# Five more score pairs on VectorE in the first five head groups of a fused attention and long-convolution kernel

## The chip, the cores and the metric

One core of one Trainium2 chip runs the whole program. The metric is the device time of one execution in microseconds; the profile gives the span of one execution of the same kernel, which is about 2 us shorter. Five engines work side by side, each on its own list of instructions that it takes strictly in order: TensorE (PE in the profile; its weight loads are PEld), ScalarE (ACT), VectorE (DVE), GpSimd (POOL) and SyncE (SP), which issues most DMA transfers. Engines wait for each other on semaphores. PSUM, where TensorE writes its results, has eight banks of 128x512 fp32.

## The reference, cut to what matters

Two branches over S = 2048 tokens with D = 640 channels are mixed by a gate. Branch B is attention with 32 query heads of 20 channels that share one key and one value head. Branch A is a short convolution of `A_k` (4 taps), a product with `A_v`, a long convolution along the 2048 tokens done as Fourier transforms, and a product with `A_q`.

```python
def _B_ref(x, wq, wk, wv, wo):
    q = (x @ wq).reshape(B, S, 32, 20)        # per head
    k, v = x @ wk, x @ wv                     # one head, shared
    p = softmax(q k^T * 20 ** -0.5)           # 32 x 2048 x 2048 scores
    return (p v).reshape(B, S, 640) @ wo

def _A_ref(q, k, v, shift_k, ssm_k, ssm_D):
    kv = short_conv4(k, shift_k) * v
    y = irfft(rfft(kv, 2S) * rfft(ssm_k, 2S))[:S] + kv * ssm_D
    return q * y

g = sigmoid((x * gate_w).sum(-1))
out = g * _A_ref(x, ...) + (1 - g) * _B_ref(x, ...)
```

The scores are 32 x 2048 x 2048 exponentials. The kernel cuts them into 2048 tiles of 128 keys x 512 queries for one head.

## The kernel before

**Groups and tiles.** A head group `G` (32 of them) is four heads for one block of 512 queries. It has 16 key blocks `j`, and each (G, j) has four tiles, one for each head `r`. A tile's scores come from one matmul with 20 (+1) channels of 32 rows, so up to four tiles with different `r` use different row strips of the array at once. ScalarE takes the exponential of three tiles (`ETA`, 128x1536) and of two tiles (`ETB`, 128x1024) by turns, out of PSUM banks 0-2 and 3-4. TensorE then multiplies the exponentials with the values (the PV matmuls, into bank 6).

**Pairs on VectorE.** In some (G, j), the list `DVE_J[G]` says which, two of the four tiles are not given to ScalarE. VectorE computes their exponentials with a polynomial on the bits of the number.

```python
SIDE = (7, 5)
DVE_J = [()] * 5 + [(3, 8, 13)] * 27
...
    def stream(self):
        tiles, self.on_dve, self.pv_order = [], {}, []
        order = (0, 1, 2, 3)
        for G in range(8 * NB):
            for j in range(NSC):
                mine = order
                if j in DVE_J[G]:
                    mine, rest = order[:2], order[2:]
                    self.on_dve[G, j] = tuple(sorted(rest))
                    order = rest + mine
                self.pv_order.append((G, j, mine))
                tiles += [(G, j, r) for r in mine]
        self.units, i = [], 0
        while i < len(tiles):
            n = 2 if len(self.units) % 2 else 3      # ETB, ETA by turns
            self.units.append(tiles[i:i + n])
            i += n
...
        def DEXP(G, j):                              # one pair on VectorE
            ...
            for h, r in enumerate(rs):
                gr = self.group("dqk", pr, banks=(5, 7))
                gr.rides = True                      # scores beside another score group
                self.mm(gr, ...score(e, bk, G, j, r)...)
                self.evac(gr, "dve", ...W <- bank * a + b...)      # L1120, 128x512, twice
            V(... X <- (w + DP) * w ...)                           # L1123, 128x1024
            V(... X <- (X + DQ) * w ...)                           # L1124, 128x1024
            V(... ETd (int16 bits) <- X * DA + W ...)              # L1126, 128x1024
...
            if j == 0:                               # in PV, after the first key block of G
                for jd in DVE_J[G]:
                    DEXP(G, jd)
                    a = PVmm(ra, jd, T["ETd"][:, 0:512], ...)
                    b = PVmm(rb, jd, T["ETd"][:, 512:1024], ...)   # both before PV of G's last j
```

`dW` has two buffers, `dX` and `ETd` have one.

**The order is made beforehand.** All operations are recorded in a graph with estimated costs. A list scheduler places them, engine by engine, when its own estimates say that the inputs, a PSUM bank and the gap until the next score group allow it; it fills gaps on TensorE with side work (projections, the short convolution, the Fourier transforms) or with dummy matmuls. What comes out is a fixed list for each engine. On the chip each engine follows its list, and waits where an estimate was too short.

```python
    def kshift(self):                                # the short convolution
        for b in range(NB):                          # 4 blocks of 512 tokens
            x = self.g.add("sp", ...e.dma_start_transpose(kTr block b, A_k block b)..., lat=1.6)  # L1293
            x.iss = 3.3
            self.dma(kv block b, A_v block b)
        ...
        for c in range(NDC):
            for q in range(NB):                      # 16 matmuls of 128x128x128 per (c, q), L1310
                ... matmul(bank, kTr[:, c, t0:t0 + 128], kdiag[:, c, j, :]) ... reads kTr blocks q and q - 1
                self.evac(gr, "dve", ...kv <- bank * kv...)
```

In the list before, the first matmul that needs the second block of `kTr` stands behind the scores of the 10th exponential; the first that needs the third block stands behind those of the 17th, and the first that needs the fourth block behind those of the 20th.

Of the kernel before, what the change touches and what calls it, by code (L numbers as in the profile page):

```python
# [541 lines left out]
UP = 256.0  # L542

SIDE = (7, 5)
DVE_J = [()] * 5 + [(3, 8, 13)] * 27
MAC_ALT = ()
SCALE = float(DH) ** -0.5

# [25 lines left out]
class Kernel:  # L574
# [451 lines left out]
    def stream(self):  # L1026
# [4 lines left out]
# [5 lines that stand above are left out]
# [11 lines left out]
    def attention(self):  # L1047
# [88 lines left out]
        def PV(G, j, rs, more=False):  # L1136
# [13 lines left out]
            if j == 0:  # L1150
                for jd in DVE_J[G]:
                    DEXP(G, jd)
# [418 lines left out]
```

## Time and profile before

| what | before |
|---|---|
| time, median of 3 | 893.52 us (893.17 to 894.32) |
| span of the profiled execution | 891.6 us |
| ScalarE busy | 868.3 us, 97% |
| TensorE busy | 855.1 us, 96% |
| VectorE busy | 658.2 us, 74% |
| GpSimd busy | 365.6 us, 41% |
| exponentials on ScalarE | 378 `ETA` and 377 `ETB`; the last `ETA` holds one tile |
| pairs on VectorE | 81 |
| dummy matmuls on TensorE (L1511) | 916, 75.8 us |

The page gives for each engine the time in which it had an instruction under way. For ScalarE the recorded start of an exponential can lie before the end of the one ahead of it, so that durations overlap (378 times a mean of 1570 ns and 377 times 1151 ns are more than the span); what one costs is the distance between ends. TensorE's share contains the dummy matmuls and matmuls that run at once in different strips.

### The profile page before, as it was taken

To read this page: it belongs to the slowest core of one execution; us is meant where nothing else is said; L and a number is where in the kernel's file an instruction comes from. 1 tells how busy PE (TensorE), PEld (TensorE's weight loads), DVE (VectorE), ACT (ScalarE), POOL (GpSimd) and SP (SyncE) were. 2 spreads that over 40 slices of the span, in tenths; PEclk is the share of its full clock that TensorE was granted. 3 is DMA by queue.
4 is the path that set the end of the run, shared out by engine and by line. 5 is a ranking of instruction groups with operands and counts; after the bars stand their busy time and mean duration, and the time that the engine had idled before them with its cause. 6 is when DMAs were issued, how large, how long until landed. Compare 5 with 4: busy or idle time off the path is not lost.

```text
span 891.6 us, 17952 instructions
## 1 busy us (share of the span) xinstructions
PE 855.1 (96%) x7801; PEld 348.9 (39%) x7825; DVE 658.2 (74%) x867; ACT 868.3 (97%) x779; POOL 365.6 (41%) x311
## 2 busy tenths in 40 slices
PE   7899999999999999999999999999999999999997
PEld 3334434433433344433333334443444443343233
DVE  6457653298778788877879877768887678878674
ACT  5899999999999999999999999999999999999995
POOL 2950057860333377244427324268512677300000
PEclk9999999999999999999999999999999999999999
DMA  7930200010000011000001010000000000300211
GB/s 158 210 128 11 67 20 15 19 31 19 21 13 20 12 28 31 20 20 14 18 10 42 20 48 23 19 9 19 19 20 19 14 14 2 101 22 29 65 43 53
DMA packets 58371, 32.62 MB, mean 37 GB/s; under 512 B 41139, under 2 KB 54324, under 8 KB 58292
## 3 DMA queue, kind: packets, MB, share of 16 engines
q1 hardware_dynamic: 56026, 30.89, 12.5%
q8 instruction: 61, 1.00, 0.5%
q10 hardware_dynamic: 2266, 0.59, 0.3%
q14 instruction: 18, 0.15, 0.1%
HBM read 17.85 MB, written 6.02 MB: 27 GB/s over the span
## 4 chain that ended last, share of the span: by engine, by line
ACT 79%; PE 17%; DMA 2%; SPq 1%; DVE 1%; issue 0%; DVEq 0%
ACT ETA L1091 47%; ACT ETB L1091 32%; PE ps L1368 5%; PE ps L1059 5%; PE ps L1131 3%; PE ps L1310 1%; PE ps L982 1%; DMA kTr<-in_A_k_dram 1%; DMA xT<-in_A_q_dram 1%; SPq L755 1%; PE ps L1434 0%; SPq L1293 0%; PE ps L1511 0%; PE ps L1249 0%; DVE ETd L1126 0%
## 5 line engine op out<-in xcount | busy, mean ns | idle before, releaser
L1091 ACT ACTIVATE ETA<-ps 128x1536 bf16<-128x1536 f32 x378 | 593.4, 1570 | 3.9 <-PE ps L1059 3.4
L1091 ACT ACTIVATE ETB<-ps 128x1024 bf16<-128x1024 f32 x377 | 433.9, 1151 | 0.1
L1401 POOL TENSOR_TENSOR Pp<-X,K 128x512 f32<-128x512 bf16 x120 | 180.2, 1528 | 373.7 <-DVE K L1389 373.6
L1059 PE MATMUL ps<-qT,kT 32*128 32x512 bf16 x2048 | 300.2, 385 | 20.4 <-ACT ETA L1091 13.1
L1059 PEld LDWEIGHTS ps<-qT,kT 32*128 32x128 bf16 x2048 | 73.8, 91 | 255.4 <-ACT ETB L1091 121.7
L1131 PE MATMUL ps<-ETA,vaug 128*32 128x512 bf16 x1132 | 152.7, 385 | 0.0
L1120 DVE TENSOR_SCALAR dW<-ps 128x512 f32<-128x512 f32 x162 | 111.3, 687 | 50.7 <-PE ps L1059 49.4
L1131 PE MATMUL ps<-ETB,vaug 128*32 128x512 bf16 x754 | 148.5, 385 | 0.1
L1126 DVE SCALAR_TENSOR_TENSOR ETd<-dX,dW 128x1024 int16<-128x1024 f32 x81 | 110.6, 1366 | 25.3 <-PE ps L1131 25.0
L1123 DVE SCALAR_TENSOR_TENSOR dX<-dW 128x1024 f32<-128x1024 uint16 x81 | 111.7, 1380 | 0.9
L1124 DVE SCALAR_TENSOR_TENSOR dX<-dX,dW 128x1024 f32<-128x1024 f32 x81 | 108.7, 1341 | 0.5
L1401 POOL TENSOR_TENSOR AB<-Pp 128x256 bf16<-128x256 f32 x80 | 82.1, 1026 | 6.0
L1434 PE MATMUL ps<-AB,Tcos 128*128 128x256 bf16 x320 | 77.3, 275 | 0.0
L1511 PE MATMUL ps<-Tcos,zeros 128*32 128x512 bf16 x916 | 75.8, 385 | 0.3
L1434 PE MATMUL ps<-AB,Tsin 128*128 128x256 bf16 x280 | 68.6, 274 | 0.0
L1401 POOL TENSOR_TENSOR Pp<-Pp 128x512 f32<-128x512 f32 x40 | 61.0, 1524 | 3.1
L1368 PE MATMUL ps<-ssm_kT,Tcos 128*128 128x256 bf16 x320 | 55.3, 276 | 0.0
L1368 PE MATMUL ps<-kv,Tcos 128*128 128x256 bf16 x320 | 50.2, 275 | 0.1
L1368 PE MATMUL ps<-ssm_kT,Tsin 128*128 128x256 bf16 x320 | 49.1, 274 | 0.0
L1368 PE MATMUL ps<-kv,Tsin 128*128 128x256 bf16 x320 | 48.4, 274 | 0.0
L1131 PEld LDWEIGHTS ps<-ETA,vaug 128*32 128x32 bf16 x1132 | 29.3, 94 | 34.9 <-issue 34.0
L982 PE MATMUL ps<-xT,wq_pad 128*128 128x512 bf16 x137 | 38.9, 382 | 2.5 <-issue 1.3
(137 smaller groups left out, 746.8 us busy)
## 6 DMA issues: line engine op xcount, KB each, us to landing
rbc<-scr_d SPq DMA_DIRECT2D x31, 256.0 KB
scr_o<-oTn SPq DMA_DIRECT2D x24, 128.0 KB, 1.7
xn<-in_A_q_dram SPq DMA_DIRECT2D x4, 640.0 KB
kv<-in_A_v_dram SPq DMA_DIRECT2D x4, 640.0 KB, 4.8
out_dram<-outsb SPq DMA_DIRECT2D x14, 160.0 KB, 1.8
oTp<-scr_o SPq DMA_DIRECT2D x12, 160.0 KB, 2.8
wog<-in_B_wo_dram SPq DMA_DIRECT2D x4, 200.0 KB
wo<-in_B_wo_dram SPq DMA_DIRECT2D x4, 200.0 KB
```

The costliest lines, as they stand in the source:

```text
L982: o = self.mm(gr, lambda e, bk, gi=gi, dc=dc: e.matmul(self.bank(bk), T["wq_pad"][:, dc, 128 * gi:128 * gi + 128], T["xT"][:, dc, 512 * I: ...
L1059: return e.matmul(self.bank(bk), T["kT4"][32 * r:32 * r + 32, 128 * j:128 * j + 128], T[f"qT{G // 8 % 2}"][32 * r:32 * r + 32, G % 8, :], ...
L1091: op("act", lambda e: e.activation(et(n)[:, 0:w], self.ps[:, lo:lo + w], ACT.Exp, scale=SCALE), [("ps", base[n % 2] + k) for k in range(le ...
L1120: self.evac(gr, "dve", lambda e, bk, h=h: e.tensor_scalar(W[:, 512 * h:512 * h + 512], self.bank(bk), SCALE * LOG2E * 128.0, 128.0 * (127 ...
L1123: V(lambda e: e.scalar_tensor_tensor(X[:, :], w, DP, w, ALU.add, ALU.mult), [kW], ["dX"], c_ps(1024), **k)
L1124: V(lambda e: e.scalar_tensor_tensor(X[:, :], X[:, :], DQ, w, ALU.add, ALU.mult), [kW], ["dX"], c_ps(1024), **k)
L1126: V(lambda e: e.scalar_tensor_tensor(T["ETd"][:, :].bitcast(dt.int16), X[:, :], DA, W[:, :], ALU.mult, ALU.add), [kW, "dX"], ["ETd"], c_ps ...
L1131: return op("pe", lambda e: e.matmul(self.bank(6)[32 * r:32 * r + 32, :], T[va][:, j, :], src, start=(j == 0), stop=(j == NSC - 1), tile_p ...
L1368: self.mm(gr, lambda e, bk, lhs=lhs, rhs=rhs, comp=comp, n=n: e.matmul(self.bank(bk, 256, 256 * comp), lhs, rhs, start=(n == 0), stop=(n = ...
L1401: f = lambda e: e.tensor_tensor(out, a, b, alu)
L1434: self.mm(gr, lambda e, bk, lhs=lhs, fc=fc, comp=comp, h=h: e.matmul(self.bank(bk, 256, 256 * h), lhs, AB[:, fc, :, comp, :], start=(fc == ...
L1511: sch.filler = [[lambda e, r=r, st=st: e.matmul(self.bank(6)[32 * r:32 * r + 32, :], self.T["zeros"][:, 0:32], self.T["Tcos"][:, 0, 0:512] ...
```

## The change

Each of the first five head groups, which had no pair on VectorE, gets one, at key block 6. The aim is to take ten of the 2048 tiles off ScalarE. Everything else in the source stays as it is; the scheduler then makes new lists for all engines.

```diff
--- before.py
+++ after.py
@@ -542,7 +542,7 @@
 UP = 256.0
 
 SIDE = (7, 5)
-DVE_J = [()] * 5 + [(3, 8, 13)] * 27
+DVE_J = [(6,)] * 5 + [(3, 8, 13)] * 27
 MAC_ALT = ()
 SCALE = float(DH) ** -0.5
 
```

The new lists hold 375 full `ETA`, one `ETA` of one tile and 375 `ETB` on ScalarE, five times five more instructions of a pair on VectorE, and the same 2048 score matmuls on TensorE. In the new TensorE list the first matmul that needs the second block of `kTr` stands behind the scores of the 12th exponential, the first that needs the third block behind those of the 16th, and the first that needs the fourth block behind those of the 20th. SyncE's list is the same up to and with the three `xn` loads behind the `kTr` transposes. The last 66 rows of the TensorE list (the last score groups and the output projection) are the same, instruction by instruction.

## Prediction, made before the run

> **What bounds the kernel now.** I read the busy shares first, then the chain that ended last, then the chain in order of time, the list of ScalarE's instructions, and at last the stages.
>
> ```profile
> PE 855.1 (96%) x7801; PEld 348.9 (39%) x7825; DVE 658.2 (74%) x867; ACT 868.3 (97%) x779; POOL 365.6 (41%) x311
> ...
> ACT 79%; PE 17%; DMA 2%; SPq 1%; DVE 1%; issue 0%; DVEq 0%
> ACT ETA L1091 47%; ACT ETB L1091 32%; PE ps L1368 5%; PE ps L1059 5%; PE ps L1131 3%; PE ps L1310 1%; PE ps L982 1%; DMA kTr<-in_A_k_dram 1%; DMA xT<-in_A_q_dram 1%; SPq L755 1%; PE ps L1434 0%; SPq L1293 0%; PE ps L1511 0%; PE ps L1249 0%; DVE ETd L1126 0%
> ```
>
> Two engines look full, but 75.8 us of TensorE are dummies, and the chain is ScalarE's exponentials for 79% of the span. From the chain in order of time, near the end:
>
> ```profile
> 845.41 1.34 ACT ETA L1091
> 846.75 0.92 ACT ETB L1091
> 847.67 1.34 ACT ETA L1091
> ```
>
> This is the pitch with nothing in the way: 1.34 us for three tiles, 0.92 for two, 2.26 for five. The 1570 and 1151 ns in the page's groups are recorded durations that overlap, so I don't use them. 377 x 2.26 = 852.0, plus the one-tile `ETA` (0.50 in the chain) is 852.5. The first exponential starts at 23.98, the chain puts the end of the last at 882.1: 858.1 us. So about 5.6 us are lost between exponentials. I followed the ends (start plus duration) of all 755 in the list of ScalarE's instructions against that pitch. The places:
>
> ```profile
> 32.94 1.53 ACT L1091 ACTIVATE ETA<-ps 128x1536 bf16<-128x1536 f32 x1
> 34.27 1.12 ACT L1091 ACTIVATE ETB<-ps 128x1024 bf16<-128x1024 f32 x1
> 37.71 1.45 ACT L1091 ACTIVATE ETA<-ps 128x1536 bf16<-128x1536 f32 x1 [2.32 <-PE ps L1059]
> 39.23 1.02 ACT L1091 ACTIVATE ETB<-ps 128x1024 bf16<-128x1024 f32 x1
> 40.56 1.45 ACT L1091 ACTIVATE ETA<-ps 128x1536 bf16<-128x1536 f32 x1 [0.31 <-PE ps L1059]
> ```
>
> Between 35 and 47 us some 3.1 us are lost (2.4 in the first gap, then 0.17, 0.42 and 0.12); between 100 and 180 about 1.3 in pieces of 0.1 to 0.2; between 460 and 740 about 0.9. A duration of 1.45 for an `ETA` is one whose scores had only just come; 1.72, seen near 80 us, is one whose scores lay ready. What made the first gap, from TensorE's instructions in order of time and from the chain:
>
> ```profile
> 35.72 1.35 PE L1310 MATMUL ps<-kdiag,kTr 128*128 128x128 bf16 x11 [1.75 <-DMA kTr<-in_A_k_dram]
> 37.00 0.61 PE L1059 MATMUL ps<-qT,kT 32*128 32x512 bf16 x3
> ```
>
> ```profile
> 27.70 7.96 DMA kTr<-in_A_k_dram
> ```
>
> TensorE, in order, came to a short-convolution matmul whose block of `kTr` had not landed; the scores of the 11th exponential stood behind it. By stage (columns: length, then busy time of PE, PEld, DVE, ACT, POOL, granted clock, DMA):
>
> ```profile
> 35.50:39.00 3.50, 3.29 (x25) 2.18 (x25) 1.07 (x2) 1.29 (x1) 3.50 (x7) 0.51 1.24 257
> ...
> 80.00:170.00 90.00, 89.23 (x816) 41.01 (x814) 43.08 (x83) 89.86 (x81) 41.03 (x39) 1.00 0.11 27
> ```
>
> After the wait TensorE ran at half clock. From 80 to 170 us ScalarE is busy throughout and TensorE has under 1 us free in 90, while VectorE is at 48%. That is the stage that gets the new pairs, and the chain of waits does run over TensorE in it; still ScalarE loses little there.
>
> [...] L1123, L1124 and L1126 have medians of 1219 to 1224 ns. [...] the same three run up to 2174 to 2176 ns, with means of 1341 to 1380. [...]
>
> **The change, part by part.**
>
> *ScalarE.* Ten tiles go: 2048 - 2 x 81 = 1886 tiles become 1876. In fives that is 377 rounds and one tile before, 375 rounds and one tile after. Two rounds less: 2 x 2.26 = 4.5 us. The rest of one tile is the same, so the end of the kernel keeps its shape. The whole of it lies on the path.
>
> *VectorE.* Five pairs more, each two evictions (L1120, 687 ns mean) and three passes at 1.22 to 1.37 us: 5.0 to 5.5 us, 25 to 27 in all, over the first 150 us or so. VectorE's work there was about half of the time (48% from 80 to 170, 78% in the busiest 20 us), so it rises to some 70%, under the 79% that it has from 190 to 880, where three pairs in a group cost ScalarE almost nothing. I count 0.
>
> *TensorE.* The same score and PV matmuls. A pair's scores ride beside another score group; its two PV matmuls (385 ns each, side by side) make a batch of their own, and I count 0.3 us for it with the break in the batches, 1.5 for five; four score groups less give about 4 x 0.3 = 1.2 back. Net near 0. But the stage from 80 to 170 is dense, so the side work is pressed into slightly less ScalarE time: I put down 0.3 us of new small losses.
>
> *The order.* The lists are made anew, and this is worth as much as the sum above is uncertain. `kTr` lands by SyncE's list, unchanged that far. Block two was issued at 27.70 and landed at 35.67, 7.96 later. Blocks three and four were issued at 32.76 and 38.19; with the same 7.96 they land at about 40.7 and 46.2 (an estimate: before, TensorE first needed them at 45.04 and 48.30, without a wait). In the new list:
> - Block two is needed behind the scores of the 12th exponential instead of the 10th, one round later: about 36 instead of 33.96. It has then landed. The gap of 2.3 us goes.
> - Block three is needed behind the 16th. Without the gap those scores are issued when the 14th exponential ends, at 23.98 + 7 x 2.24 = 39.7, so TensorE arrives at about 40.3 and waits 0.4, which the buffered scores hide.
> - Block four is needed behind the 20th: 23.98 + 9 x 2.24 = 44.1, so TensorE arrives at about 44.5 and waits about 1.7. Nine matmuls (0.6) and the scores (0.35) follow, so the 21st exponential can start at about 47.2; unhindered it would at 23.98 + 10 x 2.24 = 46.4. That is 0.8 lost, or up to 1.8 if the clock falls to half again, as it did after 1.75 us of idling. I take 1.4.
>
> So the early losses go from 3.1 to about 1.4: 1.7 gained, since the wait comes back at a later block with more slack behind it.
>
> *Sum.* 893.5 - 4.5 - 1.7 + 0.3 = 887.6; I round to 887.5.
>
> **Rivals.**
> 1. *Only the exponentials count.* The DMA wait comes back in full at block four, because the transposes set the pace of the first 46 us and not the exponentials: 893.5 - 4.5 = 889.0. For it: the wait of 1.7 that I estimate is as long as the old one, and the clock may fall. Against: a whole round of scores more stands ahead of it in ScalarE's time.
> 2. *TensorE is the bound from 80 to 170.* Then taking tiles off ScalarE there gains nothing until later, where the side work that was put off runs in place of dummies. For it: 89.23 of 90 us busy, and the chain over TensorE. Against: ScalarE lost only about 1 us in that stage, and 2.4 to 10 us of dummies stand in each 50 us afterwards. If half of the gain goes: about 890.
> 3. *VectorE comes late.* In the new list TensorE's ride-along scores and the third and fourth batch of the convolution wait for VectorE to free a bank, in the very stretch (30 to 56 us) in which GpSimd builds tables [...]. Each late bank stops TensorE and so ScalarE. Worked through on the durations above, VectorE is 2 to 3 us ahead where TensorE needs it, so I expect nothing; if it fails, 1 to 3 us, 888.5 to 890.5.
> 4. *Everything goes well*: block four lands earlier, no loss there: 893.5 - 4.5 - 3.1 = 885.9.
>
> **Range and chances.** The 4.5 us are sure to a tenth. The order adds between -3.1 and +1, the denser stage 0 to 2. So 885.0 to 890.2 should hold it 8 times in 10. Two per cent are 17.9 us; no part comes near that on either side: faster by over 2% 0.01, within 2% 0.98, slower by over 2% 0.01.
>
> **What would show it.** The 375 `ETB`, and a distance between first and last exponential that is shorter by 4.5 plus the recovered waits. ScalarE's gap near 37 us gone; a wait of TensorE for `kTr` of 1 to 2 us near 45 us in its place, with a lower granted clock after it, and under 1.8 us lost on ScalarE. VectorE's share up by about 3 points to 77%. From 80 to 170 us ScalarE busy as before. It would be wrong if ScalarE shows gaps of over 2 us in all between 50 and 180 us, behind scores that TensorE issued late, or if the wait for `kTr` takes 3 us or more again.

## The result, and the profile after

The changed kernel takes 889.02 us in the median (887.71 to 890.97, 4 executions), the kernel before 893.92 (893.17 to 895.40, 4 executions): a ratio of 0.9945, 95% interval 0.9921 to 0.9969. Two later comparisons gave 0.9940 (0.9919 to 0.9962) and 0.9953 (0.9939 to 0.9966). So it is faster by about half a per cent, and within the 2%. It lies in the predicted range, 887.5 (885.0 to 890.2).

The page of the changed kernel, busy shares and chain:

```profile
PE 851.5 (96%) x7753; PEld 348.2 (39%) x7753; DVE 674.6 (76%) x892; ACT 863.0 (97%) x775; POOL 381.6 (43%) x311
...
ACT 86%; PE 10%; DMA 2%; SPq 1%; DVE 1%; issue 0%; DVEq 0%
```

ScalarE's share of the chain went from 79% to 86%: TensorE is on it for less time. ScalarE's list at the place of the old gap, the 9th to the 12th exponential:

```profile
34.30 1.54 ACT L1091 ACTIVATE ETA<-ps 128x1536 bf16<-128x1536 f32 x1
35.63 1.12 ACT L1091 ACTIVATE ETB<-ps 128x1024 bf16<-128x1024 f32 x1
36.53 1.56 ACT L1091 ACTIVATE ETA<-ps 128x1536 bf16<-128x1536 f32 x1
37.87 1.15 ACT L1091 ACTIVATE ETB<-ps 128x1024 bf16<-128x1024 f32 x1
```

No idle time is noted, and in TensorE's list the scores of each of the four end 0.46 to 0.90 us before the exponential ahead of it does. But further on, in the same list, there is a gap that the kernel before didn't have:

```profile
112.61 1.08 ACT L1091 ACTIVATE ETB<-ps 128x1024 bf16<-128x1024 f32 x1
115.07 1.45 ACT L1091 ACTIVATE ETA<-ps 128x1536 bf16<-128x1536 f32 x1 [1.38 <-PE ps L1059]
```

and TensorE's list says why:

```profile
113.77 0.28 PE L1368 MATMUL ps<-ssm_kT,Tcos 128*128 128x256 bf16 x1 [1.28 <-DMA ssm_kT<-in_A_ssm_k_dram]
```

TensorE waits for another transposed load, `ssm_kT`, the input of the filter's spectrum. The stage from 80 to 170 us, in the columns of the prediction (length, PE, PEld, DVE, ACT, POOL, clock, DMA):

```profile
80.00:170.00 90.00, 87.46 (x833) 38.63 (x831) 55.47 (x96) 88.62 (x80) 28.84 (x27) 1.00 0.13 27
```

VectorE went from 43.08 to 55.47 us; ScalarE is down by 1.2 us, about the size of that one gap.

I split each profiled execution in three: the start of the first exponential, the stretch from there to the end of the last, and the tail. "Losses" are the sum, over all exponentials, of the distance between their ends beyond the pitch (1.344 us for three tiles, 0.917 for two), as in the prediction.

| profiled execution | first exponential | stretch | losses in it | tail | span |
|---|---|---|---|---|---|
| before | 23.98 | 858.1 | 5.1 | 9.5 | 891.6 |
| before, once more | 25.78 | 858.0 | 5.0 | 9.4 | 893.2 |
| changed | 25.35 | 851.1 | 2.7 | 9.4 | 885.9 |
| changed, second | 25.82 | 851.2 | 2.7 | 9.5 | 886.5 |
| changed, third | 23.78 | 852.8 | 4.3 | 9.5 | 886.1 |

Without losses the stretch is 853.0 before and 848.5 after. That this is 4.5 us, two rounds, follows from how losses are defined; what the profiles show is that the losses did not grow to eat the two rounds up. The first pair of spans differs by 5.7: 4.5 from the rounds, 2.4 from the losses, 1.4 back from a later start, and 0.1 to 0.2 from the tail and rounding. (The prediction's 5.6 us of losses before are 5.1 with the pitch not rounded to 2.26.)

### The profile page after: what moved, and what is told of

Its sections match the earlier page's. It is cut to its first block, busy times and chain, and to the rows that moved or that the text cites. A ratio compares the mean times of both kernels' runs of the same rounds, so it can differ in the third digit from the quotient of the medians.

```text
span 885.9 us, 17852 instructions
## 1 busy us (share of the span) xinstructions
PE 851.5 (96%) x7753; PEld 348.2 (39%) x7753; DVE 674.6 (76%) x892; ACT 863.0 (97%) x775; POOL 381.6 (43%) x311
## 4 chain that ended last, share of the span: by engine, by line
ACT 86%; PE 10%; DMA 2%; SPq 1%; DVE 1%; issue 0%; DVEq 0%
ACT ETA L1091 51%; ACT ETB L1091 35%; PE ps L1368 3%; PE ps L1059 3%; PE ps L1131 2%; DMA ssm_kT<-in_A_ssm_k_dram 1%; PE ps L1310 1%; DMA xT<-in_A_q_dram 1%; PE ps L982 1%; SPq L755 1%; PE ps L926 0%; PE ps L1249 0%; DVE ETd L1126 0%; PE ps L1511 0%; DVE outsb L1273 0%; PE ps L1258 0%
## 5 line engine op out<-in xcount | busy, mean ns | idle before, releaser
L1401 POOL TENSOR_TENSOR Pp<-X,K 128x512 f32<-128x512 bf16 x120 | 182.5, 1546 | 350.8 <-DVE K L1389 350.6
L1120 DVE TENSOR_SCALAR dW<-ps 128x512 f32<-128x512 f32 x172 | 118.1, 687 | 55.3 <-PE ps L1059 54.2
L1126 DVE SCALAR_TENSOR_TENSOR ETd<-dX,dW 128x1024 int16<-128x1024 f32 x86 | 115.3, 1340 | 25.9 <-PE ps L1131 25.7
L1123 DVE SCALAR_TENSOR_TENSOR dX<-dW 128x1024 f32<-128x1024 uint16 x86 | 119.1, 1385 | 0.8
L1124 DVE SCALAR_TENSOR_TENSOR dX<-dX,dW 128x1024 f32<-128x1024 f32 x86 | 112.8, 1312 | 0.5
L1401 POOL TENSOR_TENSOR AB<-Pp 128x256 bf16<-128x256 f32 x80 | 87.4, 1092 | 6.0
L1511 PE MATMUL ps<-Tcos,zeros 128*32 128x512 bf16 x844 | 70.6, 384 | 0.3
L1401 POOL TENSOR_TENSOR Pp<-Pp 128x512 f32<-128x512 f32 x40 | 63.4, 1584 | 3.1
L982 PE MATMUL ps<-xT,wq_pad 128*128 128x512 bf16 x160 | 48.0, 395 | 0.3 <-DVE kTr L1290 0.3
```

The costliest lines, as they stand in the source:

```text
L982: o = self.mm(gr, lambda e, bk, gi=gi, dc=dc: e.matmul(self.bank(bk), T["wq_pad"][:, dc, 128 * gi:128 * gi + 128], T["xT"][:, dc, 512 * I: ...
L1120: self.evac(gr, "dve", lambda e, bk, h=h: e.tensor_scalar(W[:, 512 * h:512 * h + 512], self.bank(bk), SCALE * LOG2E * 128.0, 128.0 * (127 ...
L1123: V(lambda e: e.scalar_tensor_tensor(X[:, :], w, DP, w, ALU.add, ALU.mult), [kW], ["dX"], c_ps(1024), **k)
L1124: V(lambda e: e.scalar_tensor_tensor(X[:, :], X[:, :], DQ, w, ALU.add, ALU.mult), [kW], ["dX"], c_ps(1024), **k)
L1126: V(lambda e: e.scalar_tensor_tensor(T["ETd"][:, :].bitcast(dt.int16), X[:, :], DA, W[:, :], ALU.mult, ALU.add), [kW, "dX"], ["ETd"], c_ps ...
L1401: f = lambda e: e.tensor_tensor(out, a, b, alu)
```

## The experiments

**The changed kernel again**, twice, unedited.

> The changed kernel once more, for the spread between executions. Theory A (two rounds of exponentials, 4.5 us, plus the wait for the second kTr block that the new order no longer has, 3.1 us, minus a new wait for ssm_kT of 1.4 us): 893.9 - 4.5 - 3.1 + 1.4 = 887.7, and single executions apart by the 1.4 us that the first scores came later in the profiled one. Theory B (only the exponentials count; the order gives and takes the same): 889.4. In the profile: the first exponential starts at either about 24.0 or about 25.4 us, and the wait for ssm_kT near 112 us is there again.

> The changed kernel beside the version without the ssm_kT wait, on one chip. Theory A (that version gains the 1.4 us of the gap on ScalarE, the rest of the 3.4 us between their medians is the start): about 888.5, executions between 886 and 892 as before.

Measured: 888.58 us (885.96 to 892.51, 7 executions) and 888.28 (887.88 to 890.02, 5). The second profile repeats the first: start 25.82, no early gap, 1.39 us lost behind the wait for `ssm_kT` (1.49 in the first profile). The third started at 23.78 and lost more there. Its wait, its stages around it, and its list of ScalarE:

```profile
112.37 0.28 PE L1368 MATMUL ps<-ssm_kT,Tcos 128*128 128x256 bf16 x1 [1.45 <-DMA ssm_kT<-in_A_ssm_k_dram]
```

```profile
110.00:114.40 4.40, 2.79 (x22) 1.20 (x19) 1.81 (x3) 2.85 (x3) 0.00 (x0) 1.00 0.65 109
114.40:117.90 3.50, 3.50 (x22) 0.95 (x20) 1.89 (x3) 2.95 (x3) 0.00 (x0) 0.51 0.00 0
```

```profile
113.67 1.45 ACT L1091 ACTIVATE ETA<-ps 128x1536 bf16<-128x1536 f32 x1 [1.55 <-PE ps L1059]
115.02 1.02 ACT L1091 ACTIVATE ETB<-ps 128x1024 bf16<-128x1024 f32 x1
116.58 1.45 ACT L1091 ACTIVATE ETA<-ps 128x1536 bf16<-128x1536 f32 x1 [0.55 <-PE ps L1059]
118.12 1.02 ACT L1091 ACTIVATE ETB<-ps 128x1024 bf16<-128x1024 f32 x1
119.65 1.45 ACT L1091 ACTIVATE ETA<-ps 128x1536 bf16<-128x1536 f32 x1 [0.51 <-PE ps L1059]
```

Here the clock was halved for 3.5 us after the wait, and 3.1 us were lost in place of 1.4. So the wait at this place cost 1.4 to 1.5 us in two profiles and 3.1 in the third.

The start is another such case. The stage from 13 to 16.5 us, first the changed kernel's first profile, then that of before:

```profile
13.00:16.50 3.50, 3.50 (x10) 1.22 (x9) 2.13 (x10) 1.95 (x4) 0.00 (x0) 0.51 0.49 95
```

```profile
13.00:16.50 3.50, 3.44 (x31) 1.72 (x29) 2.92 (x13) 2.52 (x5) 0.00 (x0) 1.00 0.59 116
```

In the first, TensorE's projections ran at half clock (0.51) after a wait of 1.91 us for `xT`, and everything began 1.4 us later; in the second the wait was 1.74 us and the clock stayed at 1.00. That isn't the change: the second profile of the kernel before, further down, has it too.

**The early wait alone, by estimate.** The scheduler is told that a `kTr` transpose lands later.

```diff
--- before.py
-   nbytes=655360, prio=14 + b, lat=1.6, after=self.crow0, name="ld_k")
+   nbytes=655360, prio=14 + b, lat=4.6, after=self.crow0, name="ld_k")
```

> The kernel before, no pair added, but the scheduler is told that a kTr transpose takes 4.6 us to land instead of 1.6, so that the matmuls of the second block stand behind the scores of the 12th exponential instead of the 10th. Theory A: the wait near 34 us and its half clock go, 893.9 - 3.1 = 890.8, perhaps 890 to 891.5. Theory B (the order is worth nothing, the early waits come back elsewhere): 893.9. If the order were most of the gain of the change: 889.

Measured: 897.31 us, ratio 1.0033 (1.0023 to 1.0042): slower. None of the three expectations held for the time. Yet the early gap is gone: the stretch is 855.4 us and the losses 2.4, so 2.7 of theory A's 3.1 us were gained. They were more than given back: the tail is 14.3 us instead of 9.5, and the start was 0.9 later (24.89). A second bound had shown itself.

**The `ssm_kT` wait by estimate.** On the changed kernel:

```diff
-   nbytes=262144, prio=base - 100, lat=1.9, name="ld_ssmk")
+   nbytes=262144, prio=base - 100, lat=5.0, name="ld_ssmk")
```

> The changed kernel, with the scheduler told that an ssm_kT transpose takes 5.0 us to land instead of 1.9, so that the first matmul that reads it stands later. Theory A: the gap of 1.4 us on ScalarE near 113 us goes, 1.4 below the changed kernel of the same call. Theory B: the stage from 80 to 170 us is bound by TensorE and takes the 1.4 back in small gaps: the same as the changed kernel. ScalarE's losses between exponentials: A about 1.2 us in all, B about 2.6.

Measured: 910.39 us, ratio 1.0181 (1.0157 to 1.0204). Losses fell to 1.2 us and the stretch to 849.7, just as theory A has it; and the tail was 32.9 us. The chain of this run, near its end, in order of time:

```profile
896.60 0.56 DVE outsb L1466
897.21 0.87 PE ps L1463 x5
898.10 0.56 DVE outsb L1466
898.71 0.87 PE ps L1463 x5
899.60 0.56 DVE outsb L1466
```

Five matmuls of the output projection, then the eviction of their bank, then the next five: 1.5 us a group, and the source gives all these groups bank 7 (`banks=(7,)`). The exponentials had ended at 876.1.

**Twice as many pairs.** On the changed kernel:

```diff
-DVE_J = [(6,)] * 5 + [(3, 8, 13)] * 27
+DVE_J = [(4, 11)] * 5 + [(3, 8, 13)] * 27
```

> Two pairs (key blocks 4 and 11) instead of one in each of the first five groups: 20 tiles fewer on ScalarE than before, 10 fewer than in the change. Theory A (ScalarE is the bound in this stage too, VectorE and TensorE have the room): another 2 x 2.26 = 4.5 us less than the changed kernel, about 884. Theory C (TensorE is the bound from 80 to 170 us, the side work is pressed together): at most half of it, 887 to 890, and ScalarE shows gaps of over 2 us in that stage.

Measured: 913.22 us, ratio 1.0210 (1.0185 to 1.0234). The stretch is 846.7 with losses of 2.7: the losses are no larger than in the change, so all four rounds, 9.0 us, came off the stretch. Its stage from 80 to 170 us:

```profile
80.00:170.00 90.00, 86.61 (x835) 35.16 (x833) 77.63 (x120) 89.31 (x81) 18.41 (x16) 1.00 0.15 27
```

ScalarE keeps 89.31 of 90 us with VectorE at 86%. Theory C, TensorE as the bound of that stage, is out. But the tail is 39.1 us, again groups of the projection. The pages show that TensorE did not lack time over the whole run: this list holds more dummy matmuls than the change's. First the change, then this run:

```profile
L1511 PE MATMUL ps<-Tcos,zeros 128*32 128x512 bf16 x844 | 70.6, 384 | 0.3
L1511 PE MATMUL ps<-Tcos,zeros 128*32 128x512 bf16 x988 | 82.2, 384 | 1.3 <-DVE acc L1189 1.2
```

**The same work in another list.** On the changed kernel, key block 4 for 6:

```diff
-DVE_J = [(6,)] * 5 + [(3, 8, 13)] * 27
+DVE_J = [(4,)] * 5 + [(3, 8, 13)] * 27
```

> The change with key block 4 instead of 6: the same 86 pairs, the same work on every engine, another list. In it 55 matmuls of the output projection (11 groups of five) stand behind the last scores, where the change has 5. Theory D (ScalarE's stretch is shorter by 4.5 us in any list, but the time is set by whichever ends last, the exponentials or the projection behind the inverse transforms; each group left over costs 1.5 us): first to last exponential about 851 us as in the change, then a tail of about 24 us instead of 9.5, about 903. Theory A without a second bound: 888.6.

Measured: 901.80 us, ratio 1.0094 (1.0072 to 1.0115). Stretch 851.1 with losses of 2.6, as in the change; tail 24.8. This is theory D nearly to the microsecond. The tails beside what the TensorE lists say, which can be read before anything runs:

| list | score tiles ahead of the last inverse-transform matmul (of 2048) | projection matmuls behind the last scores | tail |
|---|---|---|---|
| before, changed | 1870, 1870 | 5, 5 | 9.5, 9.4 |
| before, `kTr` later | 1895 | 20 | 14.3 |
| changed, key block 4 | 1944 | 55 | 24.8 |
| changed, `ssm_kT` later | 2002 | 77 | 32.9 |
| two pairs in a group | 2022 | 97 | 39.1 |

From 5 to 97 matmuls are 18.4 groups and 29.7 us: 1.6 us for each, which agrees with the 1.5 of the chain. What in the scheduler moves the inverse transforms back in all these lists stays open. Giving the projection a second bank was not tried.

**The kernel before once more**, unedited.

> The kernel before once more, one look. If the wait for the second kTr block belongs to the list and not to one execution, the gap on ScalarE of 2.3 us behind the 10th exponential is there again, between 1.5 and 3 us; the first exponential may start 1 to 2 us later or earlier than 23.98.

Measured: one execution, 895.05 us. Its gap:

```profile
37.39 1.35 PE L1310 MATMUL ps<-kdiag,kTr 128*128 128x128 bf16 x11 [1.64 <-DMA kTr<-in_A_k_dram]
```

The gap on ScalarE cost 2.31 us (2.43 in the first profile), losses are 5.0: the wait belongs to the list. The start moved to 25.78: the nine projection matmuls behind the wait for `xT` took 3.79 us, where they took 2.10 in the first profile.

**The early wait alone, in one queue.** All compute lists are left as they are; behind the scheduler, two entries of SyncE's list change places.

```diff
 SyncE's list, before:
   kTr block 1 (transpose)
+  kTr block 2 (transpose)
   kv block 1
-  kTr block 2 (transpose)
   kv block 2
```

> The kernel before with one change in SyncE's list alone: the transpose of the second kTr block is issued ahead of the load of the first kv block. TensorE's, VectorE's and ScalarE's lists are word for word those of before. Theory A (the wait for this block costs 2.4 us and its half clock 0.7): 3.1 us less than before, about 890.7; ScalarE's losses between exponentials 2 us instead of 5. Theory B (the wait is only moved, because the transposes and loads together set the pace): the same as before; a wait for the kv load or a later kTr block comes in its place.

Measured: 892.84 us, ratio 0.9989 (0.9977 to 1.0001). The wait for `kTr` is gone, and losses are 3.3 instead of 5.1; a wait for the displaced load came in its place. TensorE's list of this run:

```profile
38.28 0.40 PE L1310 MATMUL ps<-kdiag,kTr 128*128 128x128 bf16 x4 [0.50 <-DVE kv L1314]
...
41.78 0.39 PE L1059 MATMUL ps<-qT,kT 32*128 32x512 bf16 x2 [1.03 <-DVE kv L1314]
```

VectorE's eviction had to wait for the `kv` block:

```profile
40.71 1.29 DVE L1314 TENSOR_TENSOR kv<-ps,kv 128x512 bf16<-128x512 f32 x2 [1.20 <-DMA kv<-in_A_v_dram]
```

So the profile lies between the theories: of 3.1 us, 1.7 gained and 1.4 moved. In it the start was late as well (26.46), and the medians differ by only 0.7 us, an interval that touches 1. The change gained the whole 3.1: its list needs the block two exponentials later, when it has landed.

**The `ssm_kT` wait alone, in one queue.** Both halves of an `ssm_kT` tile are recorded under one name, so the second half's transpose waits for the first to land. They go to different addresses; this wait is dropped, and the spectrum matmuls wait for both halves. Compute lists unchanged.

```diff
+        sk = [o for o in sch.order["sp"] if o.name == "ld_ssmk"]
+        for first, second in ((sk[0], sk[2]), (sk[1], sk[3])):
+            for o in self.g.all:
+                if second in o.deps:
+                    o.deps.add(first)
+            second.deps.discard(first)
```

> The changed kernel with one wait less in SyncE's list: the second half of an ssm_kT tile, which is written to other addresses, no longer waits for the first half to land. All compute lists are those of the change. Theory A: TensorE's wait of 1.3 us for ssm_kT near 112 us and the gap of 1.4 us on ScalarE behind it go, 1.4 us less than the change, about 887.2, and faster than both kernels. Theory B (TensorE is the bound in that stage): no difference to the change. Against the swapped kernel before: 4.5 us less if the exponentials count in full.

> The version without the ssm_kT wait again. Theory A: 1.4 us under the changed kernel of this call when the starts are alike, so 886 to 887.5 in the median, and executions spread as widely as the changed kernel's. Theory E (the wait is longer in the executions that were not profiled, and sets their spread): 885.2 again, within 1 us, 3 us or more under the changed kernel.

Measured: 885.22 us (884.41 to 885.96), ratio to before 0.9909 (0.9887 to 0.9931), and 886.14 (884.69 to 886.91), ratio 0.9922 (0.9908 to 0.9936). In ScalarE's list of the first of these profiles there is no gap left at this place:

```profile
111.48 1.08 ACT L1091 ACTIVATE ETB<-ps 128x1024 bf16<-128x1024 f32 x1
112.49 1.45 ACT L1091 ACTIVATE ETA<-ps 128x1536 bf16<-128x1536 f32 x1
```

Losses are 1.2 and 1.5, stretches 849.7 and 849.9. On one chip it is 2.1 us under the changed kernel (886.14 to 888.28), more than the 1.4 of theory A and less than the 3 of theory E. The two executions profiled there differ by 2.4 us in span: 2.8 from the losses (4.3 to 1.5), 0.5 back from the start. That the other executions mix waits of 1.4 and of 3.1 us fits the median but is not shown. This version beats both kernels.

**Four more dummies in the wait for `xT`**, on top of that version:

```diff
+        kvn = [o for o in pe if o.name == "kvn"][20]
+        for _ in range(4):
+            f = Op("pe", sch.filler0, c_mm(512), "c", "fill", 0.0)
+            ...                      # placed ahead of kvn
```

> The version without the ssm_kT wait, and with four dummy matmuls more on TensorE where it waits for the second xT block near 10.5 us. Theory F (the first exponential starts at 24 or at 25.5 to 26.5 us according to whether the clock was halved from about 13 us on, after this wait): no half clock before the first exponential, start near 24.2 us in every execution, the slow executions go, 885 or less. If the half clock has another cause: 885 to 887.5 and the same spread as the version without it.

Measured: 885.64 us (884.77 to 886.51), ratio 0.9918 (0.9905 to 0.9932); start 23.76, no half clock (1.00 from 13 to 16.5 us). But the version without the dummies had an undisturbed start too in both its profiles (24.23, 24.33) and the same spread, so this settles nothing about the start.

## Why the prediction was right

**Rival 1, only the exponentials, 889.0.** By the median alone it fits better than 887.5. The profiles speak against it: the early 3.1 us are gone in all three of the changed kernel, and its stretch is 7.0, 6.9 and 5.3 us shorter than that of the kernel before, or 8.2 to 8.4 without the `ssm_kT` wait, where the exponentials alone give 4.5. The medians differ by 4.9 to 5.2 us and not by the 6.0 forecast. How much of that is a late start and how much the dearer wait can't be told, since only a few executions were profiled.

**ScalarE, 4.5 us.** Right: the rounds came off the stretch in full, two of them here and four with twice the pairs.

**VectorE, 25 to 27 us more, costing 0.** Right. The 25 instructions of the five new pairs took 25.5 us. The groups of these four lines grew by only 23.0 (L1120 6.8, L1123 7.4, L1124 4.1, L1126 4.7), since the other pairs got a little shorter, and the share rose to 76% instead of the 77% foretold. ScalarE shows no gap that begins with VectorE. Rival 3 is out.

**TensorE, near 0, and 0.3 us of small losses.** The first was right, the second had the wrong sign: losses other than that of the `ssm_kT` gap are 1.2 us, where the kernel before had 2.0 besides its early ones, so they fell by 0.8.

**The order, 1.7 us gained.** The sum came out nearly right and its parts didn't, so that was luck. Block two: right, the wait is gone. Block three: no wait. Block four: the step "arrives at about 44.5 and waits about 1.7" failed. In the second profile of the version without the `ssm_kT` wait, whose start (24.33) and `kTr` issue (38.83) are near those assumed, TensorE's list has

```profile
45.31 0.39 PE L982 MATMUL ps<-xT,wq_pad 128*128 128x512 bf16 x1
45.95 0.66 PE L1310 MATMUL ps<-kdiag,kTr 128*128 128x128 bf16 x9 [0.24 <-DMA kTr<-in_A_k_dram]
```

The block landed at 45.9, 7.1 us after its issue and not 7.96, and TensorE came at 45.7 and not 44.5, because projection matmuls stand ahead of it that I hadn't counted. In the changed kernel's first profile there was no wait at all. So the whole 3.1 us of the early losses went, and 1.4 to 3.1 were lost again at a place that I hadn't looked at: the list's first use of `ssm_kT`, issued at 104.74 in the changed kernel (96.52 before), behind a wait for the last `kTr` matmul. I checked the waits for `kTr` in the new lists and not the others.

One of the prediction's own signs of being wrong came up there. It named gaps of over 2 us in all between 50 and 180 us, "behind scores that TensorE issued late"; the losses there are 2.0 us in the first two profiles, at the threshold, and 3.7 in the third. Their source is the wait for the transfer, and in the third the half clock (0.51) after it, not a lack of TensorE time: in the first profile without the wait, 0.6 us is left.

**What I didn't see** is the second bound, the output projection behind the inverse transforms. I wrote that "the end of the kernel keeps its shape" because the same one tile is left over. That reason doesn't hold: one tile is left over with key block 4 as well, and there the tail is 24.8 us. The conclusion held because the last 66 rows of the two lists are the same, and it carried the prediction more than I knew. Rival 2 looked for TensorE's limit in the stage from 80 to 170 us. It lies at the end: in the lists with other settings, the side work put off came due as a tail that is 5 to 30 us longer. The chosen key block 6 gives a list in which it doesn't.

**The range.** 885.0 to 890.2 left out the start, which is worth 1.4 us by itself, and the two prices of one wait; single executions of the changed kernel went from 885.96 to 892.51.

## What to carry to other kernels

Where the order is made beforehand, a small edit is a new list, and its side effects can be larger than its purpose: compare the lists of both kernels, every DMA wait in them and what stands behind the last instruction of the bounding engine, before counting a gain. Take work off the bounding engine, but ask what its time was hiding: here four rounds less cost 19 us, since the projection then stuck out. The clean gain in this case came from removing a wait where it is made (a dependency that isn't one), which left the compute lists alone.

## What the runs showed of the hardware

TensorE's wait for `ssm_kT` was followed by 3.5 us of half clock (0.51) in the changed kernel's third profile, where it was 1.45 us long, and not in the first, where it was 1.28 (1.00 from 113.5 to 117 us). The wait for `kTr` in the kernel before was followed by it both times: after 1.75 us the clock was 0.51 from 35.5 to 39 us; in the second profile, after 1.64 us, the eleven matmuls behind the wait took 1.35 us, where eleven like them took 0.79 at 33.37 us. The waits for `xT` in the unedited start, with the first projection matmuls behind them (ten in the first line, nine in the others):

| profile | wait for `xT` | first projection matmuls | first exponential |
|---|---|---|---|
| changed | 1.91 | 4.00 | 25.35 |
| before, two entries swapped | 1.75 | 3.79 | 26.46 |
| before, once more | 1.46 | 3.79 | 25.78 |
| before | 1.74 | 2.10 | 23.98 |
| without the `ssm_kT` wait | 1.89 | 2.10 | 24.23 |
| the same, second | 1.82 | 2.10 | 24.33 |
| changed, key block 4 | 1.45 | 2.10 | 24.13 |
| changed, third | 1.55 | 2.10 | 23.78 |

So an idle stretch of under 2 us can be enough, and it isn't always; the length of the wait doesn't tell the two apart. How busy TensorE was around it hardly does either: from 10 to 13 us it was busy for 1.09 us in the changed kernel's first profile (clock 0.51 afterwards), and for 1.26 in that of the kernel before and 1.11 in the second without the `ssm_kT` wait (1.00 afterwards). What decides it is not shown.
